# Gate and up weights as packed DRAM images with one 7 KB run per partition, double-buffered second-level sums and new instruction orders, in a two-layer linear-attention and GLU kernel

## The chip, the cores and the metric

One NeuronCore of one Trainium2 chip. The metric is device time of one execution in microseconds (us). Ratios are always taken against the kernel before in the same rounds on the same chip: the mean time of one kernel's fast runs over the mean time of the other's, so not quite the ratio of the medians quoted beside it. The kernel before takes 1496.4 us (median of 3; 1496.4 to 1497.84; with a fourth run, 1496.93).

## The reference

Two blocks, each applied twice: x = x + A(LN(x)), then x = x + B(LN(x)). Shapes: S = 2048 tokens, D = 1024, F = 3584, bfloat16.

```python
# A: linear attention, 32 heads
q, k, v = split(x @ wqkv); phi = lambda t: where(t > 0, t + 1, exp(t)) + 1e-6
kv = einsum("bhsd,bhse->bhde", phi(k), v); z = phi(k).sum(s)
o  = (phi(q) @ kv) / (phi(q) . z + 1e-6);   return o @ wo
# B: gated bilinear unit
h = (x @ w_gate) * (x @ w_up);              return h @ w_down
```

## The kernel before

B is computed in two passes over halves of the tokens: a gate/up pass (28 "units": 14 column blocks of 256, gate and up in turn, two units to a "pair"), then a down stage. So the program is: attention, gate/up pass 0, down, pass 1, down, attention, pass 2, down, pass 3, down. An attention layer runs the k and q projections, then the "G products" (the input against phi(k)), the "Wp products" (the kv sums against `wo`) and the output projection. Each 2x2 block product of gate/up takes seven block products instead of eight (Strassen-Winograd); in pass 1 two of the seven, in passes 2 and 3 three of the seven, are split a second time. The weight side needs sums of blocks: first-level sums of a unit ("S", made in pass 0, stored in `s_scratch`, loaded again in passes 1 to 3) and second-level sums of a pair ("SP", made in pass 1, stored in `sp_scratch`, loaded in passes 2 and 3).

A unit's weights lie in a ring of five slots. A slot takes two loads, one of 512-byte runs straight from the weight tensor and one of the stored sums:

```python
raw = vb(o, 2048).rearrange("p (k c) -> p k c", c=256)
dma(raw, wgu_v[m][:, :, j * 256:(j + 1) * 256], r_slot(n, 0, 4096), KRR[sl])
if not (RG["first"] and ps_ == 0):
    dma(vh(o + 4096, 2048), sscr[u], r_slot(n, 4096, 8192), KRS[sl], ...)
```

All DMAs are issued by SyncE in program order; the helper that records each operation derives every wait from the byte ranges that it reads and writes.

```python
O_DOUT = RB + 28672                     # 4 KB: sums of down weights, pass 0 only
O_UT   = [RE + 6144, RB + 31744]        # 1 KB each: temporaries of the gate*up product
```

The last kilobyte of `O_DOUT` (RB+31744 to RB+32768) is the second temporary. In pass 0 VectorE also prepares the down weights: load a block into `draw`, form four sums in `dout`, store them to `t_scratch`:

```python
def wd_tick(ph):                        # called as wd_tick(1); wd_tick(0) about every 1.6 units
    j = wdn[0]
    if ph == 0 and j < NJ: wd_load(j)
    elif ph == 1 and j < NJ:
        wd_prep(j); wd_store(j); wdn[0] += 1
```

The order of instructions within a pair is a string per pass. P1A is product 1 of unit A, D2A the finishing of product 2, "21/26/27" second-level steps, R a ring load, S2+ making or loading the next pair's second-level sums, T a hook for other work:

```python
ORDER0 = "P1A P5A P6A D2A P7A D3B' R0 P1B D4A T0 P6B D3A P7B P5B T1 R1 D4B D2B"
ORDER1 = "T0 21 P1A P1B 26 P6A 41 D3B' 27 P6B S3= D2A 46 P7A D2B P7B P5A 47 R D4A D4B S2+ P5B D3A T1"
ORDER2 = "P1A 21 P1B D3A' 26 P6A 27 T0 D2A D3B' S3= D2B 41 P6B 46 P7A 31 47 P7B D4A 36 D4B P5A P5B R S2+ T1 37"
```

Of the kernel before, what the change touches and what calls it, by code (L numbers as in the profile page):

```python
# [5 lines left out]
BF16 = mybir.dt.bfloat16  # L6
# [174 lines left out]
def build_kernel(nc, A_x, A_wqkv, A_wo, B_w_gate, B_w_up, B_w_down, out):  # L181
# [15 lines left out]
    ORDER0 = "P1A P5A P6A D2A P7A D3B' R0 P1B D4A T0 P6B D3A P7B P5B T1 R1 D4B D2B"  # L197
    ORDER1 = "T0 21 P1A P1B 26 P6A 41 D3B' 27 P6B S3= D2A 46 P7A D2B P7B P5A 47 R D4A D4B S2+ P5B D3A T1"
    ORDER2 = "P1A 21 P1B D3A' 26 P6A 27 T0 D2A D3B' S3= D2B 41 P6B 46 P7A 31 47 P7B D4A 36 D4B P5A P5B R S2+ T1 37"
# [3 lines left out]
    SZ_SLOT = 8192  # L203
# [35 lines left out]
    O_DOUT = RB + 28672  # L239
    RC = take(NR * SZ_SLOT)  # L240
# [3 lines left out]
    O_A = [RC + 2 * SZ_W + i * D * 2 for i in range(2)]  # L244
# [18 lines left out]
    P = _Prog(V_SP + NJ * 64)  # L263
# [15 lines left out]
    KSP = {q: dkey("sp" + q) for q in "23"}  # L279
    KSPW = {q: dkey("spw" + q) for q in "23"}  # L280
    KDR = dkey("dr")
    KDW = dkey("dw")
# [9 lines left out]
    sscr = nc.dram_tensor("s_scratch", (2 * NJ, 128, 2048), F16, kind="Internal").ap()  # L292
# [5 lines left out]
    with ExitStack() as es:  # L298
# [285 lines left out]

        def r_slot(n, lo=0, hi=SZ_SLOT):
            o = RC + (n + 1) % NR * SZ_SLOT
            return [(o + lo, o + hi)]
# [8 lines left out]
        def sp_place(ps_, p, q):  # L596
            sz, so = (2048, 0) if q == "2" else (1024, 2048)
            return sz, so, O_X + (8 * ps_ + 6) * D * 2 if q == "2" else O_R + 12288, R(V_SP + 64 * p + so // 64, 32)

        def sp_load(ps_, p, q):  # L600
            sz, so, o, rv = sp_place(ps_, p, q)
            dma(vh(o, sz), spscr[p, :, so:so + sz], R(o, 2 * sz), KSP[q], rd=rv)

# [3 lines left out]
        def ring_issue():  # L607
# [7 lines left out]
            if u < NU:  # L615
                j, m = unit_jm(u)
                raw = vb(o, 2048).rearrange("p (k c) -> p k c", c=256)
                dma(raw, wgu_v[m][:, :, j * 256:(j + 1) * 256], r_slot(n, 0, 4096), KRR[sl])
                if not (RG["first"] and ps_ == 0):
                    dma(vh(o + 4096, 2048), sscr[u], r_slot(n, 4096, 8192), KRS[sl], rd=R(V_S + u * 32, 32))  # L620
                return
# [52 lines left out]

        def prep_s(n):
            o = r_slot(n)[0][0]
            raw = vb(o, 2048).rearrange("p (k c) -> p k c", c=256)
            sv = vh(o + 4096, 2048).rearrange("p (q k c) -> p q k c", q=4, c=128)
            a11, a12, a21, a22 = raw[:, 0:4, 0:128], raw[:, 4:8, 0:128], raw[:, 0:4, 128:256], raw[:, 4:8, 128:256]
            rr = R(o, 4096)  # L680
            rs = [R(o + 4096 + i * 1024, 1024) for i in range(4)]
            tt(sv[:, 0], a21, a22, ALU.add, rr, rs[0])
            tt(sv[:, 1], sv[:, 0], a11, ALU.subtract, rr + rs[0], rs[1])
            tt(sv[:, 2], a11, a21, ALU.subtract, rr, rs[2])
            tt(sv[:, 3], a12, sv[:, 1], ALU.subtract, rr + rs[1], rs[3])

        def store_s(n):
            u = n % NPASS
            sl = (n + 1) % NR
            dma(sscr[u], vh(r_slot(n)[0][0] + 4096, 2048), R(V_S + u * 32, 32), KSW[sl], rd=r_slot(n, 4096, 8192))  # L690
# [16 lines left out]
        def layer_A(lnp, nxt, first):  # L707
# [65 lines left out]
            for kind, i in seq:  # L773
# [9 lines left out]
                if kind == "k" and not first:  # L783
                    for t in ([tok[i - 2]] if 2 <= i < NST - 1 else tok[i - 2:] if i == NST - 1 else []):
                        dma(xr[:, t, :], nscr[t * 128:(t + 1) * 128, :], r_xr(t), KNL[t], rd=R(V_XN + t * 32, 32))
                if kind == "k" and i == NST - 1:
# [61 lines left out]
            for n in range(2 * KT):  # L848
                gchunk(n)
                if n == 2:  # L850
                    z_final()
# [48 lines left out]
            for i in range(NST):  # L900
# [14 lines left out]
                if not first and i == 12:  # L915
                    for k in range(4):
                        stash(4 + k)
# [10 lines left out]
        def layer_B(lnp, nxt, first):  # L928
# [10 lines left out]
            def pair(ps_, p, l2):  # L939
                xp = O_X + (8 * ps_ + 4) * D * 2  # L940
# [7 lines left out]
                for ab_ in range(2):  # L948
                    n = ps_ * NPASS + 2 * p + ab_
                    o = r_slot(n)[0][0]  # L950
                    raw = vb(o, 2048).rearrange("p (k c) -> p k c", c=256)
                    sv = vh(o + 4096, 2048).rearrange("p (q k c) -> p q k c", q=4, c=128)
                    rraw = R(o, 4096)
                    rs = [R(o + 4096 + i * 1024, 1024) for i in range(4)]
                    units.append(dict(j=unit_jm(2 * p + ab_)[0], n=n, w={
                        "1": (raw[:, 0:4, 0:128], rraw), "2": (raw[:, 4:8, 0:128], rraw), "3": (sv[:, 3], rs[3]), "4": (raw[:, 4:8, 128:256], rraw),
                        "5": (sv[:, 0], rs[0]), "6": (sv[:, 1], rs[1]), "7": (sv[:, 2], rs[2])}))
# [59 lines left out]
                def l2_of(q):  # L1017
# [6 lines left out]
                    else:  # L1024
                        sp = vh(o_sp["2"], 2048).rearrange("p (i k c) -> p i k c", i=4, c=256)[:, :, :, (0 if q == "2" else 128):(128 if q == "2" else 256)]
# [54 lines left out]
                def sums(q, mode):  # L1080
# [4 lines left out]
                    sp = vh(o, sz)  # L1085
                    ws = []
                    for u in units:
                        if q == "3":
                            ws.append(u["w"]["3"])
                        else:  # L1090
                            o_ = r_slot(u["n"])[0][0]
                            ws.append((vb(o_, 2048).rearrange("p (k c) -> p k c", c=256)[:, 4:8, :], R(o_, 4096)))
                    (wA, rA), (wB, rB) = ws
                    sp = sp.rearrange("p (i k c) -> p i k c", i=4, k=2)
# [313 lines left out]
```

## Time and profile before

Stage times, from the starts of the matmuls in the trace (a pass runs from its first gate/up matmul to the first down matmul after its last gate/up matmul):

| stage | before, us |
|---|---|
| attention 1 | 241.4 |
| pass 0 / 1 / 2 / 3 | 177.9 / 174.2 / 167.5 / 166.9 |
| each down stage | 83.1 |
| attention 2 | 231.4 |

Back to back, a 512-column matmul starts every 0.216 us and a 256-column one every 0.108 us; by their counts the passes need 169, 163, 160 and 160 us. (The prediction's pass times are 2 us shorter than these: they leave out the stretch at the end where the last gate/up matmuls and the first down matmuls alternate.) The page's totals, then the table by window (attention 1 and the four passes; columns are length, busy us of each engine with its instruction count, granted TensorE clock, mean DMA share, GB/s). PE is the tensor engine, PEld its weight loads, DVE VectorE, ACT ScalarE, POOL GpSimd, SPq SyncE's queue:

```profile
PE 1465.1 (98%) x7597; PEld 730.5 (49%) x7662; DVE 1152.0 (77%) x2122; ACT 538.7 (36%) x1096; POOL 217.1 (15%) x239
```

```profile
core 0: us, PE busy (x) PEld busy (x) DVE busy (x) ACT busy (x) POOL busy (x), PEclk, DMA share, GB/s
0.00:242.80 242.80, 236.58 (x1149) 109.96 (x1173) 196.94 (x338) 95.13 (x145) 109.31 (x121) 0.99 0.49 122
242.80:420.70 177.90, 172.22 (x791) 71.95 (x791) 129.81 (x290) 66.90 (x114) 2.37 (x6) 1.00 0.86 263
503.80:678.00 174.20, 169.00 (x960) 91.88 (x960) 159.87 (x367) 83.95 (x196) 6.78 (x16) 1.00 0.84 261
992.50:1160.00 167.50, 164.16 (x1043) 100.05 (x1043) 150.95 (x298) 103.57 (x254) 2.85 (x6) 1.00 0.76 234
1243.20:1410.00 166.80, 163.29 (x1043) 100.37 (x1043) 142.92 (x276) 102.07 (x252) 0.00 (x0) 1.00 0.75 241
```

PE is near full everywhere, so what can be won is the few us by which each pass exceeds its matmuls. Who waited for whom (total us, times, longest), in pass 0, then pass 1, then pass 2:

```profile
DVE arena L637 <- DMA t_scratch<-arena: 20.1, 11, 3.9
PEld ps L967 <- ACT arena L972: 15.3, 43, 1.2
...
PE ps L967 <- DVE arena L637: 3.7, 4, 1.4
```

```profile
PEld ps L967 <- issue: 6.6, 9, 1.6
DVE arena L634 <- DMA arena<-in_B_w_up_dram: 4.8, 10, 1.2
...
PE ps L967 <- DMA arena<-in_B_w_up_dram: 2.4, 5, 1.1
```

```profile
PEld ps L1040 <- issue: 3.5, 6, 1.0
PE ps L1040 <- DMA arena<-sp_scratch: 1.8, 4, 0.7
```

"arena" stands for every buffer in SBUF, "ps" for PSUM; "issue" is time in which the engine waited for nothing that the profile shows. L637 is the product `stt`, L634 the plain `tt` (which also makes the weight sums), L967 first-level and L1040 second-level matmuls. In pass 0 a product on VectorE waits for the store of down-weight sums. In pass 1 sums and matmuls wait for the up weights; in pass 2 the 256-column matmuls wait for second-level sums.

The loads of pass 2 (KB each, median us from issue to landing):

```profile
arena<-s_scratch SPq DMA_DIRECT2D x23, 512.0 KB, 6.8
arena<-sp_scratch SPq DMA_DIRECT2D x13, 512.0 KB, 4.5
arena<-in_B_w_up_dram SPq DMA_DIRECT2D x12, 512.0 KB, 4.7
arena<-in_B_w_gate_dram SPq DMA_DIRECT2D x11, 512.0 KB, 7.0
arena<-sp_scratch SPq DMA_DIRECT2D x14, 256.0 KB, 2.8
```

### The profile page before, as it was taken

What the parts mean: (1) busy time and instruction counts of PE and PEld (TensorE: products, weight loads), DVE (VectorE), ACT (ScalarE), POOL (GpSimd) and SP (SyncE); (2) the same over time, 40 slices, a digit from 0 to 9 for tenths busy, and PEclk for the clock granted to TensorE, in tenths of its full rate; (3) what the DMA queues carried; (4) which work ended last, traced back from release to release, by engine and by line L of the source; (5) the groups of instructions that cost most, each with busy time, mean ns of one, the idle gap of its engine ahead of it and who ended that gap; (6) DMA issues with size and microseconds to landing.
All of it is one profiled execution on the core that took longest, in us unless ns stands there. A gap on an engine that the chain in (4) does not pass through costs nothing.

```text
span 1496.2 us, 20408 instructions
## 1 busy us (share of the span) xinstructions
PE 1465.1 (98%) x7597; PEld 730.5 (49%) x7662; DVE 1152.0 (77%) x2122; ACT 538.7 (36%) x1096; POOL 217.1 (15%) x239
## 2 busy tenths in 40 slices
PE   8999999999999999999999999999999999999999
PEld 4444444433444455554444444445656445656544
DVE  7986978777756599986578779789888666888853
ACT  3332355433300244550023313466665004666400
POOL 4544621000000000000034346210000000000000
PEclk9999999999999999999999999999999999999999
DMA  6134666788965589976374246758777656778652
GB/s 225 36 92 112 148 135 182 220 264 262 302 225 183 205 257 274 278 239 222 124 227 127 97 116 146 195 136 263 255 250 228 227 198 208 252 244 256 229 171 100
DMA packets 317362, 295.99 MB, mean 198 GB/s; under 512 B 104144, under 2 KB 268240, under 8 KB 317264
## 3 DMA queue, kind: packets, MB, share of 16 engines
q1 hardware_dynamic: 317264, 294.70, 64.8%
q8 instruction: 60, 0.98, 0.3%
q14 instruction: 38, 0.31, 0.1%
HBM read 221.25 MB, written 49.81 MB: 181 GB/s over the span
## 4 chain that ended last, share of the span: by engine, by line
PE 75%; DVE 11%; DMA 10%; issue 2%; POOL 1%; ACT 1%; SPq 1%; DVEq 0%; ACTq 0%
PE ps L1225 23%; PE ps L967 19%; PE ps L716 15%; PE ps L1040 8%; PE ps L798 7%; DVE arena L634 5%; DMA arena<-sp_scratch 3%; DVE arena L637 2%; DMA arena<-in_B_w_up_dram 2%; DVE arena L422 2%; DMA t_scratch<-arena 2%; PE ps L884 2%; DMA arena<-arena 1%; DMA sp_scratch<-arena 1%; SPq L396 1%
## 5 line engine op out<-in xcount | busy, mean ns | idle before, releaser
L967 PE MATMUL ps<-arena 128*128 128x512 f16 x2240 | 535.5, 379 | 10.2 <-DVE arena L637 3.7
L637 DVE SCALAR_TENSOR_TENSOR arena<-ps,arena 128x512 f16<-128x512 f32 (+2 forms) x564 | 377.4, 686 | 200.7 <-PE ps L1225 144.5
L634 DVE TENSOR_TENSOR arena<-arena 128x512 f16<-128x512 f16 (+6 forms) x868 | 404.7, 493 | 50.5 <-ACT arena L1044 27.2
L1225 PE MATMUL ps<-arena 128*128 128x512 f16 (+1 forms) x1548 | 338.0, 379 | 1.1
L967 PEld LDWEIGHTS ps<-arena 128*128 128x128 f16 (+1 forms) x2240 | 212.0, 98 | 225.5 <-ACT arena L972 19.2
L1225 PEld LDWEIGHTS ps<-arena 128*128 128x128 f16 x1568 | 153.5, 98 | 184.1
L1040 PE MATMUL ps<-arena 128*128 128x256 f16 x1568 | 221.8, 273 | 7.3 <-DMA arena<-sp_scratch 4.7
L716 PE MATMUL ps<-arena 128*128 128x512 bf16 x1003 | 223.6, 381 | 3.2 <-ACT arena L526 1.1
L1040 PEld LDWEIGHTS ps<-arena 128*128 128x128 f16 (+1 forms) x1568 | 149.7, 98 | 94.2 <-ACT arena L1044 13.5
L1044 ACT ACTIVATE arena<-ps 128x256 f32<-128x256 f32 x448 | 155.3, 384 | 110.7 <-PE ps L1040 107.0
L972 ACT ACTIVATE arena<-ps 128x512 f32<-128x512 f32 x224 | 133.9, 598 | 108.2 <-PE ps L967 82.0
L568 ACT ACTIVATE arena<-ps 128x512 f32<-128x512 f32 x128 | 76.4, 597 | 234.3 <-PE ps L716 220.1
L716 PEld LDWEIGHTS ps<-arena 128*128 128x128 f16 x1024 | 100.0, 98 | 122.0 <-issue 1.6
L993 ACT COPY ps<-ps 128x512 f32<-128x512 f32 x112 | 63.8, 570 | 263.8 <-PE ps L967 263.8
L798 PE MATMUL ps<-arena 128*128 128x512 bf16 x500 | 114.6, 379 | 0.6
L884 PE MATMUL ps<-arena 128*128 128x512 bf16 x502 | 110.8, 379 | 3.5 <-ACT ps L878 2.9
L425 POOL TENSOR_SCALAR arena<-arena 128x1 f32<-128x1 f32 x64 | 21.2, 331 | 608.4 <-DVE arena L424 608.4
L422 DVE BATCH_NORM_STATS2 arena<-arena 128x6 f32<-128x512 bf16 x128 | 88.2, 689 | 12.7 <-DMA arena<-in_A_x_dram 6.1
L745 POOL TENSOR_TENSOR arena<-arena 128x1024 f16<-128x1024 f32 x32 | 79.9, 2497 | 90.2 <-DVE arena L743 84.2
L571 DVE SCALAR_TENSOR_TENSOR arena<-ps,arena 128x512 bf16<-128x512 f32 x128 | 88.5, 692 | 4.4
L569 DVE TENSOR_SCALAR arena<-arena 128x512 f32<-128x512 f32 x128 | 65.7, 513 | 28.4 <-ACT arena L568 27.2
L728 POOL TENSOR_TENSOR arena<-arena 128x512 f32<-128x512 f32 x60 | 74.7, 1248 | 87.6 <-DVE arena L571 86.1
(48 smaller groups left out, 497.1 us busy)
## 6 DMA issues: line engine op xcount, KB each, us to landing
arena<-s_scratch SPq DMA_DIRECT2D x84, 512.0 KB, 6.8
arena<-in_B_w_gate_dram SPq DMA_DIRECT2D x56, 512.0 KB, 6.9
arena<-in_B_w_up_dram SPq DMA_DIRECT2D x56, 512.0 KB, 4.6
arena<-t_scratch SPq DMA_DIRECT2D x32, 896.0 KB, 5.6
arena<-in_B_w_down_dram SPq DMA_DIRECT2D x24, 896.0 KB, 6.9
s_scratch<-arena SPq DMA_DIRECT2D x28, 512.0 KB, 6.8
arena<-sp_scratch SPq DMA_DIRECT2D x28, 512.0 KB, 4.5
arena<-in_A_wqkv_dram SPq DMA_DIRECT2D x12, 1024.0 KB, 8.5
```

Source lines behind the costliest of these rows:

```text
L422: P.add("dve", (lambda h: lambda e: e.bn_stats(st[j][:, 6 * h:6 * h + 6], x_res[:, i, (D // 2) * h:(D // 2) * (h + 1)]))(h), rd=r_x(i, (D ...
L571: P.add("dve", lambda e: e.scalar_tensor_tensor(out=dst_ap, in0=psb(bank), scalar=0.0, in1=etmp[r], op0=ALU.max, op1=ALU.add), prd=[bank], ...
L634: P.add("dve", lambda e: e.tensor_tensor(out=out, in0=a, in1=b, op=op), rd=rd, wr=wr, prd=prd)
L637: P.add("dve", lambda e: e.scalar_tensor_tensor(out=out, in0=a, scalar=sc, in1=b, op0=ALU.mult, op1=op1), rd=rd, wr=wr, prd=prd)
L716: return [e.matmul(psb(bank), xnT[:, k, i * 128:(i + 1) * 128], w[:, k, h * 512:(h + 1) * 512], start=(k == 0), stop=(k == KT - 1)) for k ...
L798: return [e.matmul(psb(bank), xr[:, t, j * 128:(j + 1) * 128], pk[:, h, t, :], start=(t == 0), stop=(t == NST - 1)) for t in range(NST)]
L884: return [e.matmul(psb(bank), xnT[:, g, i * 128:(i + 1) * 128], wp[:, g, dh * 512:(dh + 1) * 512], start=(dh == 0 and g == 0), stop=(g == ...
L967: P.add("pe", lambda e: [e.matmul(psb(bank), w[:, k, :], x[:, k, :], start=(start and k == 0), stop=(k == 3), skip_group_check=True) for k ...
L972: P.add("act", lambda e: e.activation(t, psb(bank), AF.Copy, scale=SG), prd=[bank], wr=r)
L1040: P.add("pe", lambda e: [e.matmul(psb(bank)[:, 256 * half:256 * half + 256], w[:, k, :], xx[:, k, :], start=(start and k == 0), stop=(k == ...
L1044: P.add("act", lambda e: e.activation(dst, psb(bank)[:, 0:256], AF.Copy, scale=SG), prd=[bank], wr=rd_)
L1225: return [e.matmul(psb(bank), hv[:, 7 * hf + k, t * 128:(t + 1) * 128], w[:, k, :], start=(start and hf == 0 and k == 0), stop=(hf == 1 an ...
```

## The change

Intent: copy gate and up weights once, during attention 1, into a DRAM image whose rows hold a unit's four blocks followed by its sums, so that passes 1 to 3 load a unit with one 7 KB run per partition (block 21 is only needed to make sums and is left out); give each second-level sum two buffers; retune the orders. Besides, the down-weight preparation of pass 0 is spread over two units and its output buffer is moved. The core of the diff:

```diff
-    ORDER0 = "P1A P5A P6A D2A P7A D3B' R0 P1B D4A T0 P6B D3A P7B P5B T1 R1 D4B D2B"
+    ORDER0 = "P1A P5A P6A D2A P7A D3B' P1B D4A T0 P6B R0 D3A P7B R1 P5B D4B D2B T1"
+    ORDER1 = "T0 P1A D3B' 21 P1B 26 P6A 27 P6B S3= D2A 41 D2B P5A 46 P7A 47 P7B D4A P5B R D3A D4B S2+ T1"
+    ORDER2 = "21 P1A P1B D3A' D3B' 26 S3= P6A T0 27 D2A 41 P6B D2B 46 P7A 31 47 S2+ P7B D4A 36 D4B P5A P5B 37 T1 R"
-    SZ_SLOT = 8192
+    SZ_SLOT = 7168
-    O_DOUT = RB + 28672
+    O_DOUT = O_R + 8192
+        def pack():                                    # one unit: two DRAM-to-DRAM copies of 256 KB
+            ...
+            for i in range(2):
+                c0 = j * 256 + (1 - i) * 128           # 128 columns: runs of 256 bytes
+                dma(w16[:, i], wgu_v[m][:, :, c0:c0 + 128], ...)
-                dma(raw, wgu_v[m][:, :, j * 256:(j + 1) * 256], r_slot(n, 0, 4096), KRR[sl])
-                if not (RG["first"] and ps_ == 0):
-                    dma(vh(o + 4096, 2048), sscr[u], r_slot(n, 4096, 8192), ...)
+                if RG["first"] and ps_ == 0:
+                    dma(vh(RC + sl * 1024, 512), wscr[u][:, 0:512], ...)      # block 21
+                    dma(vh(o, 1536), wscr[u][:, 512:2048], ...)
+                else:
+                    dma(vh(o, 3584), wscr[u][:, 512:4096], r_slot(n), ...)
+            o = {"2": (xp + 4096, RC), "3": (O_R + 12288, xp + 8192)}[q][p % 2]   # second buffers
+                if first and i >= 3:                   # in the k/q projections of attention 1
+                    pack()
+                if first and n < 4:                    # and in the first four G products
+                    pack()
-                        wd_prep(j)                     # old: sums, store, next load together
-                        wd_store(j)
+                    if u % 2: wd_prep(j)               # new: sums in odd units, store and load in even
+                    else:
+                        if j: wd_store(j - 1)
+                        if j < NJ: wd_load(j)
# cut: sum code on the new layout, five instead of four rows of x stashed, semaphores
```

More of the change, by code (lines that the diff above doesn't have):

```diff
@@ L196, in build_kernel @@
     L2SETS = {(False, 0): "", (False, 1): "24", (True, 0): "234", (True, 1): "234"}
-    ORDER0 = "P1A P5A P6A D2A P7A D3B' R0 P1B D4A T0 P6B D3A P7B P5B T1 R1 D4B D2B"
-    ORDER1 = "T0 21 P1A P1B 26 P6A 41 D3B' 27 P6B S3= D2A 46 P7A D2B P7B P5A 47 R D4A D4B S2+ P5B D3A T1"
-    ORDER2 = "P1A 21 P1B D3A' 26 P6A 27 T0 D2A D3B' S3= D2B 41 P6B 46 P7A 31 47 P7B D4A 36 D4B P5A P5B R S2+ T1 37"
+    ORDER0 = "P1A P5A P6A D2A P7A D3B' P1B D4A T0 P6B R0 D3A P7B R1 P5B D4B D2B T1"
+    ORDER1 = "T0 P1A D3B' 21 P1B 26 P6A 27 P6B S3= D2A 41 D2B P5A 46 P7A 47 P7B D4A P5B R D3A D4B S2+ T1"
+    ORDER2 = "21 P1A P1B D3A' D3B' 26 S3= P6A T0 27 D2A 41 P6B D2B 46 P7A 31 47 S2+ P7B D4A 36 D4B P5A P5B 37 T1 R"
     ORDERS = {(False, 0): ORDER0, (False, 1): ORDER1, (True, 0): ORDER2, (True, 1): ORDER2}
@@ L238, in build_kernel @@
     O_DRAW = O_R + 12288
-    O_DOUT = RB + 28672
-    RC = take(NR * SZ_SLOT)
+    O_DOUT = O_R + 8192
+    RC = take(NR * (SZ_SLOT + 1024) + 1024)
+    O_SLOT = RC + NR * 1024
     O_WK = RC
@@ L243, in build_kernel @@
     O_WV = RC + SZ_W
-    O_A = [RC + 2 * SZ_W + i * D * 2 for i in range(2)]
+    O_A = [RC + 2 * SZ_W + 1024 + i * D * 2 for i in range(2)]
     O_ZB = O_A[1] + D * 2
@@ L262, in build_kernel @@
     V_SP = V_D + NJ * 32
-    P = _Prog(V_SP + NJ * 64)
+    V_PK = V_SP + NJ * 64
+    P = _Prog(V_PK + 2 * NJ * 64)
     dma_keys = []
@@ L278, in build_kernel @@
     KSW = [dkey("sw%d" % i) for i in range(NR)]
-    KSP = {q: dkey("sp" + q) for q in "23"}
-    KSPW = {q: dkey("spw" + q) for q in "23"}
+    KSP = {(q, i): dkey("sp%s%d" % (q, i)) for q in "23" for i in range(2)}
+    KSPW = {(q, i): dkey("spw%s%d" % (q, i)) for q in "23" for i in range(2)}
     KDR = dkey("dr")
+    KPK = [dkey("pk%d" % i) for i in range(2 * NJ)]
     KDW = dkey("dw")
@@ L291, in build_kernel @@
     xscr = nc.dram_tensor("x_scratch", (S, D), BF16, kind="Internal").ap()
-    sscr = nc.dram_tensor("s_scratch", (2 * NJ, 128, 2048), F16, kind="Internal").ap()
+    wscr = nc.dram_tensor("w_scratch", (2 * NJ, 128, 4096), F16, kind="Internal").ap()
     spscr = nc.dram_tensor("sp_scratch", (NJ, 128, 3072), F16, kind="Internal").ap()
@@ L585, in r_slot @@
         def r_slot(n, lo=0, hi=SZ_SLOT):
-            o = RC + (n + 1) % NR * SZ_SLOT
+            o = O_SLOT + (n + 1) % NR * SZ_SLOT
             return [(o + lo, o + hi)]
@@ L597, in sp_place @@
             sz, so = (2048, 0) if q == "2" else (1024, 2048)
-            return sz, so, O_X + (8 * ps_ + 6) * D * 2 if q == "2" else O_R + 12288, R(V_SP + 64 * p + so // 64, 32)
+            xp = O_X + (8 * ps_ + 3) * D * 2
+            o = {"2": (xp + 4096, RC), "3": (O_R + 12288, xp + 8192)}[q][p % 2]
+            return sz, so, o, R(V_SP + 64 * p + so // 64, 32)
+        pk_n = [0]
+        def pack():
+            u = pk_n[0]
+            if u >= NU:
+                return
+            pk_n[0] += 1
+            j, m = unit_jm(u)
+            w16 = wscr[u].bitcast(BF16)[:, 0:2048].rearrange("p (i k c) -> p i k c", i=2, c=128)
+            for i in range(2):
+                c0 = j * 256 + (1 - i) * 128
+                dma(w16[:, i], wgu_v[m][:, :, c0:c0 + 128], R(V_PK + u * 64 + 32 * i, 32), KPK[u])
         def sp_load(ps_, p, q):
             sz, so, o, rv = sp_place(ps_, p, q)
-            dma(vh(o, sz), spscr[p, :, so:so + sz], R(o, 2 * sz), KSP[q], rd=rv)
+            dma(vh(o, sz), spscr[p, :, so:so + sz], R(o, 2 * sz), KSP[q, p % 2], rd=rv)
         def unit_jm(u):
@@ L615, in ring_issue @@
             if u < NU:
-                j, m = unit_jm(u)
-                raw = vb(o, 2048).rearrange("p (k c) -> p k c", c=256)
-                dma(raw, wgu_v[m][:, :, j * 256:(j + 1) * 256], r_slot(n, 0, 4096), KRR[sl])
-                if not (RG["first"] and ps_ == 0):
-                    dma(vh(o + 4096, 2048), sscr[u], r_slot(n, 4096, 8192), KRS[sl], rd=R(V_S + u * 32, 32))
+                if RG["first"] and ps_ == 0:
+                    dma(vh(RC + sl * 1024, 512), wscr[u][:, 0:512], R(RC + sl * 1024, 1024), KRS[sl], rd=R(V_PK + u * 64, 64))
+                    dma(vh(o, 1536), wscr[u][:, 512:2048], r_slot(n, 0, 3072), KRR[sl], rd=R(V_PK + u * 64, 64))
+                else:
+                    dma(vh(o, 3584), wscr[u][:, 512:4096], r_slot(n), KRR[sl], rd=R(V_S + u * 32, 32) + R(V_PK + u * 64, 64))
                 return
@@ L673, in tp_ops, with wt, wt_h @@
             return res
+        def wt(o):
+            return vb(o, 512).rearrange("p (k c) -> p k c", c=128)
+        def wt_h(o):
+            return vh(o, 512).rearrange("p (k c) -> p k c", c=128)
         def prep_s(n):
             o = r_slot(n)[0][0]
-            raw = vb(o, 2048).rearrange("p (k c) -> p k c", c=256)
-            sv = vh(o + 4096, 2048).rearrange("p (q k c) -> p q k c", q=4, c=128)
-            a11, a12, a21, a22 = raw[:, 0:4, 0:128], raw[:, 4:8, 0:128], raw[:, 0:4, 128:256], raw[:, 4:8, 128:256]
-            rr = R(o, 4096)
-            rs = [R(o + 4096 + i * 1024, 1024) for i in range(4)]
-            tt(sv[:, 0], a21, a22, ALU.add, rr, rs[0])
-            tt(sv[:, 1], sv[:, 0], a11, ALU.subtract, rr + rs[0], rs[1])
-            tt(sv[:, 2], a11, a21, ALU.subtract, rr, rs[2])
-            tt(sv[:, 3], a12, sv[:, 1], ALU.subtract, rr + rs[1], rs[3])
+            o21 = RC + (n + 1) % NR * 1024
+            sv = [wt_h(o + 3072 + i * 1024) for i in range(4)]
+            a11, a12, a21, a22 = wt(o + 1024), wt(o + 2048), wt(o21), wt(o)
+            r11, r12, r21, r22 = R(o + 1024, 1024), R(o + 2048, 1024), R(o21, 1024), R(o, 1024)
+            rs = [R(o + 3072 + i * 1024, 1024) for i in range(4)]
+            tt(sv[0], a21, a22, ALU.add, r21 + r22, rs[0])
+            tt(sv[1], sv[0], a11, ALU.subtract, r11 + rs[0], rs[1])
+            tt(sv[2], a11, a21, ALU.subtract, r11 + r21, rs[2])
+            tt(sv[3], a12, sv[1], ALU.subtract, r12 + rs[1], rs[3])
         def store_s(n):
@@ L689, in store_s @@
             sl = (n + 1) % NR
-            dma(sscr[u], vh(r_slot(n)[0][0] + 4096, 2048), R(V_S + u * 32, 32), KSW[sl], rd=r_slot(n, 4096, 8192))
+            dma(wscr[u][:, 2048:4096], vh(r_slot(n)[0][0] + 3072, 2048), R(V_S + u * 32, 32), KSW[sl], rd=r_slot(n, 3072, 7168))
         def wd_load(j):
@@ L915, in layer_A @@
                 if not first and i == 12:
-                    for k in range(4):
-                        stash(4 + k)
+                    for k in range(5):
+                        stash(3 + k)
                 if not first and i == 14:
@@ L939, in pair @@
             def pair(ps_, p, l2):
-                xp = O_X + (8 * ps_ + 4) * D * 2
+                xp = O_X + (8 * ps_ + 3) * D * 2
                 s0 = ps_ * 1024
@@ L950, in pair @@
                     o = r_slot(n)[0][0]
-                    raw = vb(o, 2048).rearrange("p (k c) -> p k c", c=256)
-                    sv = vh(o + 4096, 2048).rearrange("p (q k c) -> p q k c", q=4, c=128)
-                    rraw = R(o, 4096)
-                    rs = [R(o + 4096 + i * 1024, 1024) for i in range(4)]
-                    units.append(dict(j=unit_jm(2 * p + ab_)[0], n=n, w={
-                        "1": (raw[:, 0:4, 0:128], rraw), "2": (raw[:, 4:8, 0:128], rraw), "3": (sv[:, 3], rs[3]), "4": (raw[:, 4:8, 128:256], rraw),
-                        "5": (sv[:, 0], rs[0]), "6": (sv[:, 1], rs[1]), "7": (sv[:, 2], rs[2])}))
+                    w = {q: (wt(o + 1024 * i), R(o + 1024 * i, 1024)) for i, q in enumerate("412")}
+                    w.update({q: (wt_h(o + 3072 + 1024 * i), R(o + 3072 + 1024 * i, 1024)) for i, q in enumerate("5673")})
+                    units.append(dict(j=unit_jm(2 * p + ab_)[0], n=n, w=w))
                 xb = {"1": (xblk(0, s0), r_xblk(0, s0)), "2": (xblk(1, s0), r_xblk(1, s0)), "3": (xblk(1, s0 + 512), r_xblk(1, s0 + 512)),
@@ L1024, in l2_of @@
                     else:
-                        sp = vh(o_sp["2"], 2048).rearrange("p (i k c) -> p i k c", i=4, c=256)[:, :, :, (0 if q == "2" else 128):(128 if q == "2" else 256)]
+                        sp = vh(o_sp["2"], 2048).rearrange("p (i b k c) -> p i b k c", i=4, b=2, c=128)[:, :, "42".index(q)]
                         rp = [R(o_sp["2"] + i * 1024, 1024) for i in range(4)]
@@ L1085, in sums @@
                     sp = vh(o, sz)
+                    nb = sz // 1024
                     ws = []
                     for u in units:
-                        if q == "3":
-                            ws.append(u["w"]["3"])
-                        else:
-                            o_ = r_slot(u["n"])[0][0]
-                            ws.append((vb(o_, 2048).rearrange("p (k c) -> p k c", c=256)[:, 4:8, :], R(o_, 4096)))
+                        o_ = r_slot(u["n"])[0][0]
+                        if q == "2":
+                            ws.append((vb(o_, 2048).rearrange("p (b i k c) -> p b i k c", b=2, i=2, k=2)[:, :, 0], R(o_, 3072)))
+                        else:
+                            ws.append((vh(o_ + 6144, 512).rearrange("p (b k c) -> p b k c", b=1, k=2), R(o_ + 6144, 1024)))
                     (wA, rA), (wB, rB) = ws
-                    sp = sp.rearrange("p (i k c) -> p i k c", i=4, k=2)
+                    sp = sp.rearrange("p (i b c) -> p i b c", i=4, b=nb)
                     rp = [R(o + i * sz // 2, sz // 2) for i in range(4)]
-                    tt(sp[:, 0], wB[:, 0:2], wB[:, 2:4], ALU.add, rB, rp[0])
-                    tt(sp[:, 1], sp[:, 0], wA[:, 0:2], ALU.subtract, rp[0] + rA, rp[1])
-                    tt(sp[:, 2], wA[:, 0:2], wB[:, 0:2], ALU.subtract, rA + rB, rp[2])
-                    tt(sp[:, 3], wA[:, 2:4], sp[:, 1], ALU.subtract, rp[1] + rA, rp[3])
-                    dma(spscr[p, :, so:so + sz], vh(o, sz), rv, KSPW[q], rd=R(o, 2 * sz))
+                    tt(sp[:, 0], wB[:, :, 0], wB[:, :, 1], ALU.add, rB, rp[0])
+                    tt(sp[:, 1], sp[:, 0], wA[:, :, 0], ALU.subtract, rp[0] + rA, rp[1])
+                    tt(sp[:, 2], wA[:, :, 0], wB[:, :, 0], ALU.subtract, rA + rB, rp[2])
+                    tt(sp[:, 3], wA[:, :, 1], sp[:, 1], ALU.subtract, rp[1] + rA, rp[3])
+                    dma(spscr[p, :, so:so + sz], vh(o, sz), rv, KSPW[q, p % 2], rd=R(o, 2 * sz))
                 def fin(q, c):
@@ L1185, in tail @@
                         ring_issue()
-                    for t in range(4):
-                        i = 8 * ps_ + 4 + t
+                    for t in range(5):
+                        i = 8 * ps_ + 3 + t
                         dma(x_res[:, i, :], xscr[i * 128:(i + 1) * 128, :], r_x(i), KX[i], rd=R(V_X + i * 32, 32))
@@ L1270, in layer_B, with wd_tick @@
             if first:
-                wdn = [0]
-                def wd_tick(ph):
-                    j = wdn[0]
-                    if ph == 0 and j < NJ:
-                        wd_load(j)
-                    elif ph == 1 and j < NJ:
-                        wd_prep(j)
-                        wd_store(j)
-                        wdn[0] += 1
+                def wd_tick(u):
+                    j = u // 2
+                    if u % 2:
+                        wd_prep(j)
+                    else:
+                        if j:
+                            wd_store(j - 1)
+                        if j < NJ:
+                            wd_load(j)
             def ticks0(u):
@@ L1284, in ticks0 @@
                     lnp.flush_step()
-                if first and wdn[0] < NJ and wdn[0] * 22 <= (u - 3) * NJ:
-                    wd_tick(1)
-                    wd_tick(0)
+                if first and u:
+                    wd_tick(u)
             def dticks0(q, t):
                 if q == "2" and t == 3:
-                    for k in range(4):
-                        stash(12 + k)
+                    for k in range(5):
+                        stash(11 + k)
                 if q == "6" and t == 3 and not first:
@@ L1333, in layer_B @@
             if first:
-                for k in range(4):
-                    stash(4 + k)
+                for k in range(5):
+                    stash(3 + k)
             tail = gateup(0, ticks0, L2SETS[not first, 0])
+            if first:
+                wd_tick(2 * NJ)
             lnp.need(NST - 1)
@@ L1369, in build_kernel @@
         layer_B(lnB, None, False)
-        P.plan({KOUT})
+        P.plan({KOUT} | set(KPK))
         P.emit(nc, block, esem, dsem, [KOUT])
```

## The prediction

> **What bounds the kernel now.** The tensor engine. The page gives PE 98% busy and a granted clock of 0.999. Back to back, a 512-column matmul takes 0.216 us and a 256-column one 0.108 us (read from matmul starts in the trace). Counting matmuls by line, the four gate/up passes need 169, 163, 160 and 160 us; the trace gives them 175.7, 172.0, 165.5 and 164.9. So all four lose about 25 us together. The down stages (about 85 us each) and both attention layers (about 242 and 232 us, ideal about 230) have little to lose apart from the start. The change aims only at those 25 us.
>
> **What ends those waits (waits view by stage window).** Pass 1 (172 us): the weight sums and the tensor engine wait for the up-weight load (4.8 and 2.4 us directly, and 6.6 us of "issue" idle of the weight loads that goes with it); VectorE is 91% busy there. Passes 2 and 3: the 256-column matmuls wait for the load of second-level sums (1.8 and 2.9 us, plus 3.3 to 3.5 us "issue"); the chain of waits names the same loads. Pass 0: VectorE waits 20.1 us for the store of transformed down weights, in its program order, and holds the tensor engine about 6.5 us.
>
> **What the change does.**
> - Removes, per unit in passes 1 to 3, one load of 1024 512-byte packets and one of 128 4 KB packets (29 and 175 ns a packet: about 3.3 us of all 16 DMA engines); adds 128 packets of 7 KB (332 ns: about 2.7 us). DMA share in the passes should fall from 74-87% by about 10 points, and loads land in 5-6 us instead of up to 7.5.
> - Double buffers the second-level sums, so they are requested earlier; new instruction orders. Pass 0 separates down-weight load, sums and store by one unit each, which should take most of VectorE's 20 us wait away.
> - VectorE operation count is unchanged.
> - Adds 56 DRAM-to-DRAM copies of 256 KB in the first attention layer: 57,344 runs of 256 bytes, 3,584 an engine. DMA is nearly idle there from 27 to 100 us (14 to 28% share), so there is room. But between two DMA transposes, 6.9 us apart, two units are packed: 256 packets an engine. The trace has no 256-byte copy from DRAM to DRAM; loads' medians (27 ns at 512 B, 46 at 1 KB) extrapolate to about 18 ns, an estimate, so 4.6 us plus 1.5 us of transpose: just fits. [...]
>
> **Critical path.** Gain in gate/up: about 3 + 4 + 3 + 2 = 12 us of the 25; pass 1 keeps several because VectorE is nearly full. First attention layer: 0 expected, a mean of perhaps 3 us with the tail.
>
> **Prediction: 1485 us**, 80% range 1471 to 1500. Faster by over 2%: 0.02; within 2%: 0.92; slower by over 2%: 0.06.
>
> **What would show it.** Matmul time of pass 1 near 167 us, passes 2 and 3 near 162, pass 0 near 172; waits for up-weight loads and sum loads gone from the tensor engine; VectorE's wait for the down-weight store under 5 us; DMA share over 80% from about 30 to 115 us, without new tensor-engine gaps before the transposed blocks; first attention layer still about 242 us.
>
> **What would make it wrong.** 256-byte DRAM-to-DRAM packets above about 22 ns: transposes queue behind packs, gaps in the k/q projections, late v and o weights. Or the pass-1 loss is VectorE's own order, and nothing is gained there. Or new orders expose PSUM or buffer waits.

The sum: 1496.4 us before, less 12 in the passes, plus 0 (expected) to 3 (mean with the tail) in attention 1, comes to 1484.4 to 1487.4.

## The result

1485.85 us (median of 4; 1484.54 to 1488.85) against 1496.93: ratio 0.9928, 95% interval 0.9911 to 0.9945, so less than 2% but clearly faster. In a later set (after_again below) the same kernel gave 0.9956 (0.9942 to 0.997). By stage, from the matmul starts:

| stage | before | after | difference | predicted |
|---|---|---|---|---|
| attention 1 | 241.4 | 247.2 | +5.8 | 0 to +3 |
| pass 0 | 177.9 | 171.3 | -6.6 | -3 |
| pass 1 | 174.2 | 170.6 | -3.6 | -4 |
| pass 2 | 167.5 | 164.3 | -3.2 | -3 |
| pass 3 | 166.9 | 163.1 | -3.8 | -2 |
| attention 2 | 231.4 | 230.5 | -0.9 | 0 |
| down stages | 83.1 each | 83.1 each | 0 | 0 |

The passes gained 17.2 us where 12 were predicted, and attention 1 lost 5.8 where 0 to 3 were predicted. The total is right partly because these two errors cancel. The page's totals and the same windows after:

```profile
PE 1462.0 (99%) x7597; PEld 730.2 (49%) x7662; DVE 1148.6 (77%) x2122; ACT 538.7 (36%) x1096; POOL 214.2 (14%) x239
```

```profile
0.00:248.50 248.50, 237.05 (x1149) 109.17 (x1173) 197.83 (x338) 95.01 (x145) 106.98 (x121) 1.00 0.79 178
248.50:419.80 171.30, 170.88 (x791) 72.34 (x791) 130.99 (x290) 66.89 (x114) 2.58 (x6) 1.00 0.86 274
502.90:673.50 170.60, 168.88 (x960) 91.19 (x960) 159.18 (x367) 84.42 (x196) 6.37 (x16) 1.00 0.74 247
987.10:1151.40 164.30, 163.15 (x1044) 100.53 (x1044) 148.34 (x298) 102.84 (x254) 2.43 (x6) 1.00 0.65 217
1234.50:1397.60 163.10, 162.52 (x1044) 100.82 (x1044) 140.46 (x276) 101.71 (x252) 0.00 (x0) 1.00 0.65 223
```

The DMA share fell by 10 points in passes 1 to 3, as predicted, and rose from 0.49 to 0.79 in attention 1, where the copies run. (In this kernel L967 has become L991, L1040 L1064, L637 L655, L634 L652, L716 L740.) The waits: in pass 0 no line for `t_scratch` is left at all, and what remains on the tensor engine is

```profile
PEld ps L991 <- ACT arena L996: 13.6, 43, 0.3
...
PE ps L991 <- DVE arena L652: 0.4, 1, 0.4
```

in pass 1 the load wait shrank from 2.4 to 0.5 us, and the sums' wait for it is gone:

```profile
PE ps L991 <- DMA arena<-w_scratch: 0.5, 2, 0.3
```

and in pass 2 nothing waits for `sp_scratch`. Yet only the larger loads of sums land sooner, 3.6 us after issue instead of 4.5; the smaller ones land later, 6.9 us instead of 2.8:

```profile
arena<-w_scratch SPq DMA_DIRECT2D x23, 896.0 KB, 6.3
arena<-sp_scratch SPq DMA_DIRECT2D x13, 512.0 KB, 3.6
...
arena<-sp_scratch SPq DMA_DIRECT2D x13, 256.0 KB, 6.9
```

The longer time to landing cost nothing here, since nothing waits for these loads. In attention 1, from 40 us on, the tensor engine now waits for DMA transposes of the normalised input (first two lines) and, at the end, for VectorE in the Wp products (L864):

```profile
PEld ps L740 <- DMA arena<-arena: 5.0, 7, 1.9
PE ps L740 <- DMA arena<-arena: 2.2, 3, 1.4
PEld ps L864 <- DVE arena L871: 1.8, 1, 1.8
PE ps L864 <- DVE arena L871: 1.5, 1, 1.5
```

Before the change the same view has no wait of the tensor engine for a transpose, and 0.4 us at the Wp products.

### The profile page after: what moved, and what is told of

Its sections match the earlier page's. It is cut to its first block, busy times and chain, and to the rows that moved or that the text cites. A ratio compares the mean times of both kernels' runs of the same rounds, so it can differ in the third digit from the quotient of the medians.

```text
span 1483.7 us, 20453 instructions
## 1 busy us (share of the span) xinstructions
PE 1462.0 (99%) x7597; PEld 730.2 (49%) x7662; DVE 1148.6 (77%) x2122; ACT 538.7 (36%) x1096; POOL 214.2 (14%) x239
## 4 chain that ended last, share of the span: by engine, by line
PE 79%; DVE 11%; DMA 5%; issue 2%; POOL 1%; ACT 1%; SPq 0%; DVEq 0%; ACTq 0%; POOLq 0%
PE ps L991 29%; PE ps L1250 23%; PE ps L740 13%; PE ps L1064 10%; DMA arena<-arena 3%; PE ps L824 3%; DVE arena L652 2%; DVE arena L760 2%; DVE arena L425 2%; DVE arena L763 2%; DVE arena L655 1%; POOL arena L769 1%; DMA arena<-w_scratch 1%; PE ps L912 1%; DVE arena L765 1%
## 5 line engine op out<-in xcount | busy, mean ns | idle before, releaser
L991 PE MATMUL ps<-arena 128*128 128x512 f16 x2240 | 530.5, 379 | 1.3 <-DMA arena<-w_scratch 0.5
L655 DVE SCALAR_TENSOR_TENSOR arena<-ps,arena 128x512 f16<-128x512 f32 (+2 forms) x564 | 373.7, 685 | 191.9 <-PE ps L1250 144.5
L652 DVE TENSOR_TENSOR arena<-arena 128x512 f16<-128x512 f16 (+6 forms) x868 | 398.8, 493 | 46.2 <-ACT arena L1068 31.6
L991 PEld LDWEIGHTS ps<-arena 128*128 128x128 f16 (+1 forms) x2240 | 213.1, 98 | 214.8 <-ACT arena L996 13.6
L740 PE MATMUL ps<-arena 128*128 128x512 bf16 x1003 | 222.8, 379 | 5.9 <-DMA arena<-arena 2.2
L1064 PE MATMUL ps<-arena 128*128 128x256 f16 x1568 | 219.0, 273 | 2.3 <-ACT arena L1068 1.9
L1064 PEld LDWEIGHTS ps<-arena 128*128 128x128 f16 (+1 forms) x1568 | 149.0, 98 | 87.4 <-ACT arena L1068 13.6
L740 PEld LDWEIGHTS ps<-arena 128*128 128x128 f16 x1024 | 99.1, 98 | 125.0 <-DMA arena<-arena 5.0
```

The costliest lines, as they stand in the source:

```text
L652: P.add("dve", lambda e: e.tensor_tensor(out=out, in0=a, in1=b, op=op), rd=rd, wr=wr, prd=prd)
L655: P.add("dve", lambda e: e.scalar_tensor_tensor(out=out, in0=a, scalar=sc, in1=b, op0=ALU.mult, op1=op1), rd=rd, wr=wr, prd=prd)
L740: return [e.matmul(psb(bank), xnT[:, k, i * 128:(i + 1) * 128], w[:, k, h * 512:(h + 1) * 512], start=(k == 0), stop=(k == KT - 1)) for k ...
L991: P.add("pe", lambda e: [e.matmul(psb(bank), w[:, k, :], x[:, k, :], start=(start and k == 0), stop=(k == 3), skip_group_check=True) for k ...
L1064: P.add("pe", lambda e: [e.matmul(psb(bank)[:, 256 * half:256 * half + 256], w[:, k, :], xx[:, k, :], start=(start and k == 0), stop=(k == ...
```

## The experiments

Twelve kernels in three sets of four; each set ran on one chip and shared its runs of the kernel before. Stage times are of the profiled run of each:

| kernel | ratio to before | attn 1 | pass 0 | pass 1 | pass 2 | pass 3 |
|---|---|---|---|---|---|---|
| before | 1 | 241.4 | 177.9 | 174.2 | 167.5 | 166.9 |
| after | 0.9928 | 247.2 | 171.3 | 170.6 | 164.3 | 163.1 |
| b_plus_packs | 1.0062 | 248.7 | 177.6 | 173.7 | 167.5 | 165.7 |
| a_old_wd | 0.9943 | 249.0 | 171.4 | 170.4 | 164.4 | 163.1 |
| a_single | 1.0556 | 247.4 | 171.9 | 170.5 | 211.3 | 208.4 |
| a_old_orders | 1.0056 | 249.0 | 176.5 | 180.6 | 164.3 | 163.1 |
| b_order0 | 1.0062 | 241.6 | 185.4 | 175.0 | 167.5 | 165.6 |
| a_single_old12 | 0.9984 | 246.9 | 172.1 | 177.7 | 164.3 | 163.1 |
| b_double | 0.9993 | 242.5 | 184.2 | 170.5 | 164.8 | 163.1 |
| a_s2 | 0.9947 | 244.4 | 175.3 | 170.7 | 164.3 | 163.1 |
| after_again | 0.9956 | 249.9 | 172.0 | 170.9 | 164.3 | 163.1 |
| b_new_wd_order0 (wrong) | 0.9969 | 242.4 | 171.1 | 175.0 | 167.0 | 167.5 |
| b_double_wd (wrong) | 0.9896 | 241.1 | 171.7 | 170.5 | 164.6 | 163.1 |
| a_s3 | 0.9892 | 244.3 | 171.9 | 170.8 | 164.3 | 163.1 |

Passes that a variant leaves as they were show how far one profile can be trusted: in the four kernels with the old orders, loads and buffers there, pass 1 took 173.7 to 175.0 us, pass 2 167.0 to 167.5 and pass 3 165.6 to 167.5.

### b_plus_packs: the copies alone

```diff
# on the kernel before: pack() and its calls as in the change; nobody reads the image
+                if first and i >= 3:
+                    pack()
+                if first and n < 4:
+                    pack()
```

> The kernel before plus the 56 copies into the packed images, which nothing reads. Theory (the copies cost the first attention layer about 5.7 us: transposes and then the normalisation transposes queue behind them): first attention layer 247 us instead of 241.6, the four passes unchanged within 1 us, total 1501 to 1503 us, ratio to before about 1.004. Rival (the 5.7 us come from moved buffers, the packed loads or the new orders, not from the copies): first layer stays at 242, ratio within 0.001 of 1.

Measured 1507.3 us (1502.81 to 1510.43), ratio 1.0062 (1.0046 to 1.0079). Attention 1 took 248.7 us, the passes stayed within 1.2 us. The theory holds: the copies alone cost what attention 1 lost. (The median lies above the expected 1501 to 1503.) They cost more in most runs than in the profiled one, so the size is not fixed: the seven profiled kernels that place the copies as the change does show attention 1 at 246.9 to 249.9 us.

### a_old_wd: the old schedule of the down weights on the kernel after

```diff
-                if first and u:
-                    wd_tick(u)
+                if first and wdn[0] < NJ and wdn[0] * 22 <= (u - 3) * NJ:
+                    wd_tick(1)
+                    wd_tick(0)
# and wd_tick as before; O_DOUT stays where the change put it
```

> The kernel after with the old schedule of the down-weight transform (sums, store and next load together). Theory (pass 0 gained by the new schedule): pass 0 back to 174 to 176 us, VectorE again waits about 20 us for the store, total 1490 to 1492. Rival (pass 0 gained by the packed loads, which leave the DMA freer, so the store lands in time): pass 0 under 171 us, total within 2 us of 1485.8.

Measured 1489.41 us, ratio 0.9943 (0.9927 to 0.9958). Pass 0 took 171.4 us and VectorE did not wait for the store once. So the new schedule is not what freed pass 0, and the theory falls. The rival as worded does not fit either: the store lands no sooner. Minimum, median and maximum for the store to `t_scratch`, before and then here:

```profile
DMA to landing us min/median/max: 3.2/3.4/6.9
```

```profile
DMA to landing us min/median/max: 3.2/3.5/5.7
```

With the same schedule and the same landing time a wait of 20.1 us is gone. The one thing left that ties a VectorE product to that store is its operand: the product's temporary shared its kilobyte with the fourth of the sums being stored, and the change moved the sums (`O_DOUT = O_R + 8192`). In the kernel before, each store had to be read out before the next product of unit B could be written. The traces bear this out. A product that goes through that temporary is followed at once on VectorE by the multiplication that uses it, so it can be told from the others: there are 28 in pass 0, two to a pair. All 11 waits for the store fall on those 28, and none on the other L637 products; it is the same for the 13 waits of b_plus_packs and the 8 each of b_order0 and b_double. The other experiments fit this: the four that run the old schedule with the sums at their old place show the wait (before 20.1, b_plus_packs 27.1, b_order0 22.2, b_double 22.9 us). The move alone on the kernel before was not run.

### a_old_orders: the old orders on the kernel after

```diff
-    ORDER0, ORDER1, ORDER2 = new strings
+    ORDER0, ORDER1, ORDER2 = strings of the kernel before
```

> The kernel after with the three instruction orders of before. Theory (orders are a fine tuning on top of buffers and runs): 1 to 4 us longer in all, 1487 to 1490. Rival (the orders made the gain in passes 1 to 3): passes 1 to 3 together about 10 us longer, total about 1496.

Measured 1505.6 us, ratio 1.0056 (1.0036 to 1.0075): 1.3% slower than the kernel after, far above the theory's range, and slower than the kernel before. But not where the rival said: passes 2 and 3 are unchanged, pass 0 loses 5.2 us and pass 1 loses 10. In pass 1 the weight sums and the matmuls wait for the packed loads, more than in the kernel before:

```profile
PEld ps L991 <- issue: 14.4, 12, 2.8
DVE arena L652 <- DMA arena<-w_scratch: 14.0, 12, 2.5
PE ps L991 <- DMA arena<-w_scratch: 8.7, 8, 2.4
```

The sums of the next pair (S2+) read what the ring load (R) has just asked for. With the old order VectorE first reaches them 4.2 to 4.7 us after that load's issue in most pairs, in the kernel before, here and in a_single_old12 alike; with the new order it reaches them after 5.8 to 6.7 us (after, b_double). The load itself, which brings the up weights, landed 4.6 us after issue (median of pass 1) as a separate 512 KB load and 5.4 us after it as a packed one of 896 KB. So in the old order the short load is a little late, the packed load later still, and in the new order either is mostly in time. In pass 0 the old order ends with the tensor engine waiting 2.9 us for VectorE before the down stage.

### a_single: one buffer for each second-level sum

```diff
-            o = {...}[q][p % 2]
+            o = {...}[q][0]
-            dma(..., KSP[q, p % 2], ...)
+            dma(..., KSP[q, 0], ...)
```

> The kernel after with one buffer and one semaphore for each of the second-level sums, all else kept. Theory (double buffering gained passes 2 and 3, 3.3 and 3.8 us, and little in pass 1): passes 2 and 3 together 5 to 7 us longer, waits of the 256-column matmuls for sp_scratch back, total 1490 to 1493. Rival (the gain came from fewer, longer DMA runs): passes 2 and 3 together less than 2 us longer, total under 1488.

Measured 1581.14 us, ratio 1.0556. Neither theory: passes 2 and 3 grew by 47 and 45 us. The experiment was badly made. The new ORDER2 puts S2+, the load of the *next* pair's sums, ahead of D4A, which still reads this pair's. With one buffer D4A then waits for that load to land each time, and by its order it even reads the wrong pair's sums (this is read from the code); the comparison with the reference passed, so it does not see this. In both passes together:

```profile
  PEld ps L1064: 77.3, 26
  PE ps L1064: 70.0, 26
```

(who waited for loads from `sp_scratch`). What it shows is that the new ORDER2 cannot do without the second buffer. It does not show what the second buffer gains. (Behind its stalls, 2.7 us in the mean by these sums, the clock was lower too: 0.987 granted over the run, 0.66 from 1150.6 to 1154.0 us.) The fair form is next.

### a_single_old12: one buffer, with the old orders of passes 1 to 3

```diff
# on a_single: ORDER1 and ORDER2 of the kernel before, ORDER0 of the change
```

> The kernel after with single buffers for the second-level sums and, so that no sum is overwritten before it is read, the old orders of passes 1 to 3 (the fair form of the single-buffer test). Theory (double buffering made the gain of passes 2 and 3): they go back from 164.3 and 163.1 to about 167.5 and 167. Rival (7 KB runs made it): they stay at 164 and 163. Pass 1: about 180 if the packed loads are what makes the old order slow there, about 174 as before if the second buffer is.

Measured 1492.99 us, ratio 0.9984 (0.9971 to 0.9996). Passes 2 and 3 are 164.3 and 163.1: with packed loads, neither second buffer nor new order is needed there. The rival (long runs) holds. Pass 1 is 177.7, between the two expectations: slower than before by 3.5 us with packed loads and one buffer, by 6.4 with two (a_old_orders).

### b_double: second buffers and new orders, no packing

```diff
# on the kernel before: the three new orders; seven rows of x stashed to make room
+            xp = O_X + (8 * ps_ + 1) * D * 2
+            o = {"2": (xp + 4096, xp + 8192), "3": (O_R + 12288, xp + 12288)}[q][p % 2]
```

> The kernel before with all three new orders and double-buffered second-level sums (seven rows of x stashed for the space), but no packed images: 512-byte loads and separate loads of the sums as before. Theory (orders and second buffer make the gains; packing only costs its copies): first attention layer 241.5, passes 171, 171 to 172, 164, 163, total about 1480, ratio about 0.989. Rival (the long runs make the gain of passes 1 to 3): pass 1 over 173, passes 2 and 3 over 166 us, total 1487 or more.

Measured 1495.24 us, ratio 0.9993 (0.9979 to 1.0007). Passes 1 to 3 are as good as after the change (170.5, 164.8, 163.1), on 512-byte loads: the long runs are not needed there either. So in passes 2 and 3 there are two cures, each enough alone: packed loads, or earlier requests into a second buffer (with the new order, which needs it). In pass 1 the order is the cure: every kernel with the new ORDER1 shows 170.4 to 170.9, whatever its loads and buffers. But the total is 15 us above the expectation, nearly all of it in pass 0 (184.2). See b_order0.

### b_order0: only the order of pass 0

```diff
-    ORDER0 = "... R0 P1B D4A T0 P6B D3A P7B P5B T1 R1 D4B D2B"
+    ORDER0 = "... P1B D4A T0 P6B R0 D3A P7B R1 P5B D4B D2B T1"
```

> The kernel before with nothing changed but the first order string (pass 0). Theory, new since the old down-weight schedule left pass 0 fast: the order of pass 0 alone made its gain; pass 0 falls from 177.9 us (first gate/up matmul to first down matmul) to 171 to 172, ratio to before about 0.996. Rival: the order needs the packed loads; pass 0 stays above 176 and the ratio at 1.

Measured 1505.73 us, ratio 1.0062 (1.005 to 1.0075). Pass 0 became 7.5 us longer. The new order alone is a loss, so neither theory nor rival. VectorE's wait for the store is 22.2 us, in 8 pieces instead of 11, and twice more than 3.4 us pass from the start of one matmul to the start of the next. One such place in order of time (start, length, engine, what, count, idle before it and its releaser):

```profile
326.88 0.69 DVE L637 SCALAR_TENSOR_TENSOR arena<-ps,arena 128x512 f16<-128x512 f32 x1 [2.70 <-DMA t_scratch<-arena]
...
327.67 0.60 ACT L972 ACTIVATE arena<-ps 128x512 f32<-128x512 f32 x1 [4.22 <-DVE arena L637]
...
328.32 14.00 PE L967 MATMUL ps<-arena 128*128 128x512 f16 x51 [3.05 <-ACT arena L972]
```

The product waits for the store, ScalarE for the product, the tensor engine for ScalarE. And after the gap the clock is halved:

```profile
322.00:328.00 6.00, 2.71 (x12) 0.84 (x10) 3.23 (x9) 1.48 (x3) 0.00 (x0) 0.94 1.00 249
328.00:334.00 6.00, 5.68 (x14) 2.04 (x15) 3.52 (x9) 0.86 (x2) 0.00 (x0) 0.50 1.10 351
334.00:340.00 6.00, 6.00 (x29) 2.51 (x27) 4.15 (x11) 2.36 (x4) 0.00 (x0) 0.99 0.24 91
```

In the middle window the granted clock is 0.50 and 14 matmuls run instead of about 28, 0.43 us apart (their ends are modelled, so PE still reads as busy). Gaps between matmul starts of 3.43 and 3.47 us were each followed by such a stretch: the granted clock was 0.83 over 320 to 340 us and 0.83 over 380 to 400 us, and 63 and 68 matmuls ran there where 94 ran from 340 to 360 us at a clock of 1.00. Behind the first gap the matmuls stayed 0.43 us apart for 5.9 us. So this stall cost more than itself, about 2.8 us more (an estimate: 13 matmuls at 0.43 us instead of 0.216). In the kernel before, the longest gap in a pass is 1.74 us, and the granted clock is 1.00 in every pass. The down stage of a_old_orders, 84.8 us instead of 83.1, begins behind a gap of 3.29 us, and there too the clock was lower: 0.77 from 424 to 430 us, 0.94 from 430 to 436 us. How long a gap has to be for this was not shown.

### b_new_wd_order0 and b_double_wd: the same two with the new down-weight schedule (wrong results)

```diff
# on b_order0 and on b_double: wd_tick as in the change; O_DOUT left at RB + 28672
```

> The kernel before with the new order of pass 0 and the new down-weight schedule, nothing packed. Theory (what pass 0 needs is that VectorE's transform doesn't wait for the store of the one before it; either the new schedule or the lighter packed loads gives that): the two stalls of 3.4 us and the half-clock stretches behind them are gone, pass 0 is 171 to 173 us instead of 185.4, total about 1490 to 1492, ratio about 0.996. Rival (pass 0 needs the packed loads themselves): pass 0 over 176, ratio at least 1.0.

> All parts of the change but the packing: new orders, second buffers, new down-weight schedule, on the loads of before. Theory: as the run with second buffers and new orders, with pass 0 at 171 to 173 instead of 184.2: total 1481 to 1484, faster than the kernel after by 2 to 5 us, because no copies are made. Rival (packed loads carry the gain of pass 0): pass 0 over 176, total 1487 or more.

Measured 1493.24 us (ratio 0.9969) and 1481.57 us (ratio 0.9896), with pass 0 at 171.1 and 171.7. Both give wrong results, with the same relative error of 0.062. By the code, in the new schedule the sums lie in `dout` for a whole unit before they are stored, and at the old place a product of unit B writes over the last kilobyte in the meantime. Nothing races, because every wait is kept; the order itself is wrong. So the new schedule *needs* the moved buffer, and with the old place it hides the wait by giving up the data. The times say that pass 0 reaches 171 us on short loads once the products hardly wait for a store (1.6 and 1.3 us, once each), and that the parts without packing would reach about 1481; but these are times of wrong kernels, and a mended one was not run.

### a_s2 and a_s3: the copies spread out

```diff
# a_s3, on the kernel after: where pack() is called (28 units in all)
-                if first and i >= 3:
+                if first and (kind == "k" and i < NST - 1 and i >= 3 or kind == "q" and (i in (3, 5, 9) or i >= 4 and i % 2 == 0)):
                     pack()
+                if first and kind == "k" and i in (3, 4):       # two more ahead of the first DMA transpose
+                    pack()
-                if first and n < 4:
-                    pack()
+                if first and n in (0, 8):                       # G products
+                    for _ in range(3 if n == 0 else 1):
+                        pack()
+                if first and i in (2, 4):                       # output projection
+                    pack()
# a_s2: 20 units in the projections, 4 in the G products (n % 4 == 3), 4 in the output projection (i % 4 == 3)
```

> The kernel after with the copies spread out: five units ahead of the first DMA transpose, one and a half for each later transpose instead of two, four in the G products, four in the output projection. Theory (the cost in the first attention layer is queueing behind the copies): first layer back from 247 to 242 or 243 us, total 1480 to 1482, ratio about 0.990. Rival (the cost is the traffic itself, wherever it is put): still 246 to 248, 1485.

> The kernel after with the copies spread out and none late in the output projection (where they made the first transposes of pass 0 late, 3.5 us, with the clock granted at 0.87 behind it). Theory: first attention layer 243 to 245, pass 0 171.5, total 1481 to 1484. Rival (traffic itself costs): first layer 246 or more, total 1486.

a_s2: 1488.63 us, ratio 0.9947 (0.9934 to 0.9959), short of what was expected. Attention 1 fell to 244.4, between theory and rival, but the copies late in the output projection held up the first transposes of pass 0: a gap of 3.47 us at its start, a clock of 0.55 behind it (from 249.8 to 252.8 us), pass 0 at 175.3. The gain was given back.

a_s3: 1482.03 us (1479.47 to 1483.77), ratio 0.9892 (0.9875 to 0.991), with attention 1 at 244.3, as its theory had it. The kernel after, in the same rounds on the same chip, had 1491.2 (1488.88 to 1492.37), ratio 0.9956:

> The kernel after, unchanged, so that the versions below are compared with it on the same chip: ratio to before 0.992 to 0.994, about 1486 us.

after_again came out slower than expected of it. Its attention 1 took 249.9 us, and there VectorE's lateness at the Wp products grew to a gap of 4.43 us, again with a lower clock behind it (0.63 granted from 188.3 to 191.3 us, matmuls 0.43 us apart):

```profile
188.31 1.17 PE L864 MATMUL ps<-arena 128*128 128x512 bf16 x4 [4.05 <-DVE arena L841]
189.28 3.49 PE L740 MATMUL ps<-arena 128*128 128x512 bf16 x8
```

Eight matmuls take 3.49 us there instead of about 1.9. In a_s3 that gap is 0.76 us; what is left of attention 1's excess (244.3 against 241.4) is mainly one wait of 2.1 us for a transpose. The same copies, the same bytes, placed elsewhere, cost 2.9 us instead of the 5.5 to 8.5 of the seven profiles above (against 241.4 of the kernel before): about half of the cost or more is queueing, not traffic. a_s3 is correct and beats both kernels.

## Why the prediction was right

- *The bound and the room.* Right: only the passes' 25 us over their matmul time could be won, and 17 of them were.
- *Passes 2 and 3 (-3 and -2 predicted, -3.2 and -3.8 measured).* Right in the wait that goes, and in size for pass 2; pass 3 gained nearly twice the forecast, of which the spread of one profile (165.6 to 167.5 us on unchanged code) may be a part. The DMA share fell by 10 points as forecast; the packed loads landed after 6.3 us, not 5 to 6. That packing and double buffering are each enough alone was not foreseen.
- *Pass 1 (-4 predicted, -3.6 measured).* Right in size, and the waits for up-weight loads went. The cause was mis-stated: the new order does it. Packed loads with the old order make pass 1 slower, 177.7 to 180.6 us, because a packed load lands 0.8 us later than the short one and the old order already asked for it too late.
- *Pass 0 (-3 predicted, -6.6 measured).* The wait was read rightly from the trace, its cause was not. The step that failed: "Pass 0 separates down-weight load, sums and store by one unit each, which should take most of VectorE's 20 us wait away." The old schedule left pass 0 at 171.4. The wait came with a kilobyte shared between the stored sums and a product's temporary, and went with one line that moves the sums. Once it is gone the new order is worth 5 us (176.5 to 171.3); with the wait in place the same order costs 7.5. Nor are 20 us of waits worth much by themselves: without them, but with the old order, pass 0 is only 1.4 us shorter (177.9 to 176.5, packed loads included).
- *Attention 1 (0 expected, perhaps 3 with the tail; 5.8 measured, 8.5 in the later set).* The mechanism was named, the size was too small. The 256-byte copies ran near the estimated 18 ns while little else ran (18.1 ns mean a packet between 20 and 40 us, from the packet records; the medians of longer packets in the kernel before, 27 ns at 512 B, 46 at 1 KB, 84 at 2 KB, 159 at 4 KB and 272 at 7 KB, lie on a line of about 8.4 ns plus 0.0368 ns a byte, which gives 17.8 ns at 256 B), but not under load: from 60 to 110 us the median of all 256-byte packets, those of the transposes included, stayed at 18 ns, while the mean was 22.3 ns, because a twentieth of the packets took 23% of the time. Two units of copies and a transpose, 320 packets an engine, then need about 7.1 us (an estimate from this mean) where the prediction summed 6.1, and a transpose was due every 6.9 us. So little or none of the slack was left, and the queue was full: DMA share 0.98 to 1.01 from 60 to 110 us, and the transposes issued from 27 to 100 us landed 5.4 us after issue instead of 3.0 (medians). Three times the tensor engine waited for a late transpose, and it was 2.3 us behind by the end of the projections. The larger part was not foreseen: the later copies and the v and o weights, ahead of them in SyncE's order, also delayed the normalisation's transposes (the first is issued at 141.5 us instead of 135.1), so VectorE arrived late at the Wp products, 3.5 us more.
- *The total.* Right, 1485 predicted and 1485.85 measured, with two errors of about 5 us that cancel, which is luck.

Left open: the move of `O_DOUT` by itself on the kernel before, and a correct kernel with all parts but the packing.

## What to carry to other kernels

Read which instruction waits, not only for what: a product that waits for a store of something else points to shared bytes, and moving a buffer may remove a wait for which the schedule seems to blame. A preparation step that uses an idle DMA queue must leave room between the small transfers that others wait for; here the same copies cost 5.5 to 8.5 us or 2.9 us by placement alone. Parts of a tuned change are not additive: here the same order gained 5 us without the wait on a shared kilobyte and lost 7.5 us with it, so test parts both by removing them and by adding them.
